# A fused attention and feed-forward kernel: the first sequence's attention written out in steps of two heads, with value copies behind exponentials and idle transposes between

## The chip, the cores and the metric

The kernel runs on one core of one Trainium2 chip. The metric is the device time of one execution in microseconds (us), lower is better. A core has five engines that concern us: TensorE (PE in the profile, with its weight loads as PEld), VectorE (DVE), ScalarE (ACT), GpSimd (POOL) and SyncE (SP). In the traces of the stage that is changed here, the instructions of each engine stand in the order in which the kernel writes them (TensorE's, from 39.51 us on, are shown below), and they wait for other engines by semaphores. "Granted clock" is the share of full speed that the throttle grants TensorE.

## The reference

Eight sequences, eight heads, 576 tokens, head size 64, all in fp32. Scores below the row's maximum minus tau are dropped before the softmax. The result goes through a feed-forward block of 512 to 2048 to 512 with an ELU between.

```python
scores = scale * np.matmul(q, k.transpose(0, 1, 3, 2))
thresh = np.max(scores, axis=-1, keepdims=True) - tau
scores = np.where(scores >= thresh, scores, -1000000000.0)
attn = np.exp(scores - np.max(scores, axis=-1, keepdims=True))
attn = attn / (np.sum(attn, axis=-1, keepdims=True) + 1e-09)
x = (attn @ v)            # then (B,H,S,D) -> (B*S, H*D)
h = x @ w_in
y = np.where(h > 0, h, np.exp(np.minimum(h, 0)) - 1) @ w_out
```

The weights arrive as float64 and are converted on the chip, piece by piece, with integer operations on VectorE, ScalarE and GpSimd.

## The kernel before

The change touches only the first sequence, which is computed before any feed-forward matmul can start. Its eight heads are four pairs of two, and a pair has five steps: four with 128 query rows of each of two heads, and a fifth with the 64 remaining rows of both heads in one tile. For every step there are scores on TensorE, a maximum on VectorE, a bias, an exponential on ScalarE, a mask on VectorE that also sums the row, and a normalising on GpSimd. Then TensorE transposes the weights (in parts, each copied out of PSUM by ScalarE), and multiplies them with the values, twice a pair. Before the change, this ran one head after another:

```python
def exponentials(pr, i, hs):
    ...
    nc.vector.tensor_reduce(st["mx"][:, cs], src[:, :, :, :HALF], axis=AX.XY, op=ALU.max)
    nc.gpsimd.tensor_scalar(st["nb"][:, cs], st["mx"][:, cs], nkeep, 1.0, ALU.mult, ALU.mult)
    ...
        nc.scalar.activation(e, st[h][:, :, :HALF], AF.Exp, bias=st["nb"][:, h : h + 1], scale=keep)

heads = [(pr, i, [h]) for pr, i in steps[:per_seq] for h in heads_of(i)]
begin(*heads[0])                              # scores and exponential
for n, (pr, i, hs) in enumerate(heads):
    if n + 1 < len(heads):
        begin(*heads[n + 1])                  # of the next head
    ...                                       # conversions of weights
    finish(pr, i, hs)                         # mask and normalise
    if len(turned) > 1:
        behind(*turned.popleft())             # values, when complete
    if n and hs == [0]:
        turn(*heads[n - 1][:2])               # transposes and their copies
        ...
```

Two pools in PSUM matter. Three buffers hold scores. Two banks, called rt, are shared by the transposed parts, by the products with the values (pv), and, in the changed kernel, by the idle transposes:

```python
def room():
    return psum["t"].tile([P, NC, P], FP32, name="rt", tag="rt")
# turn_parts of a two-head step: part 0 (4 chunks of one head), part 1 (4 chunks of the other), part 2 (the common chunk)
return [lambda: chunks(0, NC), lambda: chunks(NC + 1, NCH), lambda: chunks(NC, NC + 1)]
...
pv = psum["t"].tile([P, 512], FP32, name="pv", tag="rt")       # values: 2 passes with vd, then 16 with vm
```

## Time and profile before

| | |
|---|---|
| time, median of 3 (range) | 1388.53 us (1387.4 to 1390.45) |
| span in the profile, granted clock | 1384.1 us, 0.994 |
| first scores, first mask | 8.21 us, 13.13 us |
| scores of step 21, and their maximum | 105.55 us, 106.82 us |
| from that maximum to the end of the span | 1277.3 us |

The 21st step is the first one that both kernels write alike, so the start of its maximum is a marker: what stands before it belongs to the change, and what stands after should move as one block. I use this marker in every profile below. A timeline line gives start, duration, engine, source line, operation, output and inputs, shapes and count; in square brackets is how long the engine was idle before and what ended that.

### The profile page before, as it was taken

To read this page: it belongs to the slowest core of one execution; us is meant where nothing else is said; L and a number is where in the kernel's file an instruction comes from. 1 tells how busy PE (TensorE), PEld (TensorE's weight loads), DVE (VectorE), ACT (ScalarE), POOL (GpSimd) and SP (SyncE) were. 2 spreads that over 40 slices of the span, in tenths; PEclk is the share of its full clock that TensorE was granted. 3 is DMA by queue.
4 is the path that set the end of the run, shared out by engine and by line. 5 is a ranking of instruction groups with operands and counts; after the bars stand their busy time and mean duration, and the time that the engine had idled before them with its cause. 6 is when DMAs were issued, how large, how long until landed. Compare 5 with 4: busy or idle time off the path is not lost.

```text
span 1384.1 us, 21954 instructions
## 1 busy us (share of the span) xinstructions
PE 1334.5 (96%) x6566; PEld 988.6 (71%) x6566; DVE 1066.5 (77%) x2362; ACT 632.4 (46%) x1387; POOL 827.5 (60%) x1331
## 2 busy tenths in 40 slices
PE   6897989999999999999999999999999999999998
PEld 4554745747777777777777777777777777888886
DVE  6877885988888887888788978888888874545533
ACT  4666654325454445445453636263635452422421
POOL 5667773878657564756475747675666656414422
PEclk9999999999999999999999999999999999999999
DMA  5245451688897979898888988897889785411211
GB/s 114 58 91 148 132 148 44 187 244 254 226 261 221 280 214 255 209 266 240 230 231 256 251 222 236 236 258 212 239 230 275 217 241 146 133 58 64 92 57 31
DMA packets 316342, 259.82 MB, mean 188 GB/s; under 512 B 208320, under 2 KB 272320, under 8 KB 316224
## 3 DMA queue, kind: packets, MB, share of 16 engines
q1 hardware_dynamic: 316224, 258.42, 67.4%
q8 instruction: 53, 0.87, 0.3%
q14 instruction: 65, 0.53, 0.1%
HBM read 167.84 MB, written 90.51 MB: 187 GB/s over the span
## 4 chain that ended last, share of the span: by engine, by line
PE 76%; DVE 9%; ACT 5%; POOL 4%; issue 3%; DMA 1%; SPq 1%; DVEq 0%; POOLq 0%; ACTq 0%
PE f L999 28%; PE f L846 21%; PE sc L238 11%; PE pv L388 9%; PE pv L384 2%; PE f L435 2%; PE f L475 2%; ACT e L1088 2%; DVE w L265 2%; ACT e L253 1%; DVE mx L1078 1%; PE rt L277 1%; POOL wtop L143 1%; DVE mx L248 1%; DVE wtop L137 1%
## 5 line engine op out<-in xcount | busy, mean ns | idle before, releaser
L274 POOL TENSOR_SCALAR w<-w,rs 128x576 f32<-128x576 f32 x288 | 246.2, 860 | 108.4 <-DVE rs L1104 75.1
L1078 DVE TENSOR_REDUCE mx<-sc 128x1 f32<-128x576 f32 x207 | 148.0, 751 | 82.6 <-PE sc L238 82.6
L238 PE MATMUL sc<-kT,qT 64*128 64x288 f32 x1024 | 182.6, 440 | 22.1 <-DVE w L265 11.9
L348 DVE STREAM_TRANSPOSE x<-w 128x512 f32<-128x512 f32 (+1 forms) x350 | 182.5, 567 | 8.2 <-POOL w L274 8.2
L1086 ACT ACTIVATE nb<-mx,nkeep 128x1 f32<-128x1 f32 x207 | 61.4, 297 | 253.4 <-DVE mx L1078 253.4
L1088 ACT ACTIVATE e<-sc,nb,keep 128x576 f32<-128x576 f32 x207 | 172.1, 831 | 6.9
L1097 DVE SCALAR_TENSOR_TENSOR w<-sc,th,e 128x576 f32<-128x576 f32 x207 | 163.0, 810 | 8.6 <-ACT e L1088 0.4
L238 PEld LDWEIGHTS sc<-kT,qT 64*128 64x128 f32 x1024 | 100.7, 191 | 87.2 <-issue 51.8
L846 PE MATMUL f<-xt,sw 128*128 128x256 f32 x512 | 129.0, 389 | 1.0 <-DVE ot L1017 0.5
L846 PE MATMUL f<-xt,w_in_sb 128*128 128x256 f32 x512 | 125.1, 383 | 1.7 <-ACT w L860 1.5
L1082 POOL TENSOR_SCALAR th<-mx,ntau 128x1 f32<-128x1 f32 x207 | 54.3, 263 | 111.6 <-DVE mx L1078 111.4
L846 PEld LDWEIGHTS f<-xt,sw 128*128 128x128 f32 x512 | 93.2, 190 | 29.8 <-issue 13.5
L846 PE MATMUL f<-x,w_in_sb 128*128 128x256 f32 x448 | 109.0, 382 | 5.5 <-ACT g L913 5.5
L253 ACT ACTIVATE e<-sc,nb,keep 128x576 f32<-128x576 f32 x81 | 65.1, 830 | 104.2 <-POOL nb L249 103.2
L846 PEld LDWEIGHTS f<-xt,w_in_sb 128*128 128x128 f32 x512 | 95.7, 190 | 22.1 <-ACT xs L400 4.6
L999 PE MATMUL f<-w_out_sb,s 128*128 128x256 f32 x448 | 109.4, 387 | 0.0
L999 PE MATMUL f<-t,s 128*128 128x256 f32 x448 | 106.7, 381 | 0.6 <-POOL s L939 0.6
L999 PE MATMUL f<-w_out_sb,g 128*128 128x256 f32 x448 | 107.2, 382 | 0.0
L846 PEld LDWEIGHTS f<-x,w_in_sb 128*128 128x128 f32 x448 | 84.1, 190 | 21.2 <-ACT g L913 10.2
L999 PEld LDWEIGHTS f<-w_out_sb,s 128*128 128x128 f32 x448 | 82.3, 190 | 23.0 <-issue 13.2
L999 PEld LDWEIGHTS f<-w_out_sb,g 128*128 128x128 f32 x448 | 84.0, 190 | 15.8 <-ACT ge L879 3.5
L999 PEld LDWEIGHTS f<-t,s 128*128 128x128 f32 x448 | 84.0, 190 | 14.3 <-POOL s L939 3.4
(162 smaller groups left out, 2543.6 us busy)
## 6 DMA issues: line engine op xcount, KB each, us to landing
there<-x SPq DMA_DIRECT2D x500, 144.0 KB, 4.2
wTb<-there SPq DMA_DIRECT2D x75, 576.0 KB, 4.6
wTa<-there SPq DMA_DIRECT2D x50, 576.0 KB, 4.3
sw<-win_sums SPq DMA_DIRECT2D x62, 384.0 KB, 4.7
t<-wout_sums SPq DMA_DIRECT2D x45, 512.0 KB, 5.4
qm<-in_q_dram SPq DMA_DIRECT2D x128, 72.0 KB, 4.2
vm<-in_v_dram SPq DMA_DIRECT2D x64, 128.0 KB, 4.2
wst<-in_moe_w_in_dram SPq DMA_DIRECT2D x16, 512.0 KB, 4.5
```

The source lines that it names most:

```text
L238: nc.tensor.matmul(scs[h][:, a, :HALF], qs[r], kT[r, k0 : k0 + HALF], start=True, stop=True)
L253: nc.scalar.activation(e, st[h][:, :, :HALF], AF.Exp, bias=st["nb"][:, h : h + 1], scale=keep)
L274: nc.gpsimd.tensor_scalar(wv, wv, st["rs"][:, h : h + 1], 1.0, ALU.mult, ALU.mult)
L348: nc.vector.transpose(x[:, :, c0 : c0 + nc_], src.rearrange("p (c g n) -> p g c n", c=nc_, n=T))
L388: nc.tensor.matmul(pv[h * D : (h + 1) * D, g0 * T : g1 * T], vm[:, h, c], wT[:, g0:g1, h * (NC + 1) + c], start=False, stop=(c == NC - 1), ...
L846: nc.tensor.matmul(loc["banks"][place], left[:, j], right[:, j], start=(begins and j == 0), stop=(j == 1), skip_group_check=True)
L999: nc.tensor.matmul(place(m), lhs, rhs, start=(begins and v == 0), stop=(v == RU - 1), skip_group_check=True)
L1078: nc.vector.tensor_reduce(st["mx"][:, h : h + 1], st[h][:, :, :HALF], axis=AX.XY, op=ALU.max)
L1082: nc.gpsimd.tensor_scalar(st["th"][:, h : h + 1], st["mx"][:, h : h + 1], 1.0, ntau, ALU.mult, ALU.add)
L1086: nc.scalar.mul(st["nb"][:, h : h + 1], st["mx"][:, h : h + 1], nkeep)
L1088: nc.scalar.activation(e, st[h][:, :, :HALF], AF.Exp, bias=st["nb"][:, h : h + 1], scale=keep)
L1097: nc.vector.scalar_tensor_tensor(wv, sc[:, :, :HALF], st["th"][:, h : h + 1], e, ALU.is_ge, ALU.mult, accum_out=st["sm"][:, h : h + 1])
```

## The change

The intent is to take the waits between engines out of the first stage. The stage is now written in a fixed order by steps of two heads. The biases of the first heads go to ScalarE. The copies of the values' products and of the transposed parts stand behind the exponentials, so that ScalarE starts these first. TensorE gets idle transposes, which transpose the identity into a buffer nobody reads, to keep its clock up: 28 at the start, then 6 and 9 in three of the five steps. The first loads of k are issued by ScalarE beside those of q by SyncE. The core of it (`...` marks what is left out):

```diff
-    for n, (pr, i, hs) in enumerate(heads):
-        if n + 1 < len(heads):
-            begin(*heads[n + 1])
...
+        load(0, ("km",), queue=nc.scalar)
...
+        def idle(n):
+            rt = psum["t"].tile([P, NC, P], FP32, name="rt", tag="rt")
+            for _ in range(n):
+                transpose(rt[:, 0], ident)
+
+        idle(28)
...
+            if n:
+                normalize(*steps[n - 1], [0])
+                turned = turn_parts(*steps[n - 1])
+                if i in (0, 1, 3):
+                    idle(6)
+            max_of(pr, i, 0)
+            exp_of(pr, i, 0)
+            bound_of(pr, i, 0)
+            if n:
+                copies = turned[0]()
...
+                exp_of(pr, i, 1, True)
+                bound_of(pr, i, 1)
+            if out_values:
+                out_values()
+            if n and i < NB - 1:
+                copies()
...                                   (conversions, q and k of the next pair)
+            mask_of(pr, i, 0)
+            if i in (0, 1, 3):
+                idle(9)
+            if n + 1 < per_seq:
+                scores(*steps[n + 1], heads_of(steps[n + 1][1]))
+            if n:
+                for part in turned[1:]:
+                    part()()
+            if len(hs) == 2:
+                mask_of(pr, i, 1)
+            reciprocal_of(pr, i, hs)
+            out_values = None
+            if n > 1 and steps[n - 2][1] in (1, NB - 1):
+                out_values = values(steps[n - 2][0], 0 if steps[n - 2][1] == 1 else 1)
```

So TensorE's line in a step n is: 6 idle, part 0 of step n-1, 9 idle, scores of step n+1, parts 1 and 2 of step n-1, and in the second and fourth step of a pair, last, the values of the step before that. The idle ones are there in a pair's first, second and fourth steps.

More of the change, by code (lines that the diff above doesn't have):

```diff
@@ L78, with read_tau @@
     tau_sb = const.tile([P, 1], FP32, name="tau_sb")
-    nc.sync.dma_start(tau_sb, tau.to_broadcast([P, 1]))
-    pos = const.tile([P, 1], FP32, name="pos")
-    nc.vector.tensor_scalar(pos, tau_sb, 0.0, None, ALU.is_ge)
-    keep = const.tile([P, 1], FP32, name="keep")
-    nc.vector.tensor_scalar(keep, pos, SCALE, None, ALU.mult)
-    nkeep = const.tile([P, 1], FP32, name="nkeep")
-    nc.vector.tensor_scalar(nkeep, pos, -SCALE, None, ALU.mult)
-    far = const.tile([P, 1], FP32, name="far")
-    nc.vector.tensor_scalar(far, pos, -FAR, FAR, ALU.mult, ALU.add)
-    ntau = const.tile([P, 1], FP32, name="ntau")
-    nc.vector.tensor_tensor(ntau, tau_sb, far, ALU.max)
-    nc.vector.tensor_scalar(ntau, ntau, -1.0 / SCALE, None, ALU.mult)
+    pos, keep, nkeep, far, ntau = (const.tile([P, 1], FP32, name=x) for x in ("pos", "keep", "nkeep", "far", "ntau"))
+    def read_tau():
+        nc.vector.tensor_scalar(pos, tau_sb, 0.0, None, ALU.is_ge)
+        nc.vector.tensor_scalar(keep, pos, SCALE, None, ALU.mult)
+        nc.vector.tensor_scalar(nkeep, pos, -SCALE, None, ALU.mult)
+        nc.vector.tensor_scalar(far, pos, -FAR, FAR, ALU.mult, ALU.add)
+        nc.vector.tensor_tensor(ntau, tau_sb, far, ALU.max)
+        nc.vector.tensor_scalar(ntau, ntau, -1.0 / SCALE, None, ALU.mult)
     w_in_sb = const.tile([P, KJ, DF], FP32, name="w_in_sb")
@@ L131, in convert_top, with convert_shift @@
     def convert_top(i):
+        convert_shift(i)
+        convert_sign(i)
+    def convert_shift(i):
         if i in staged:
@@ L136, in convert_top, with convert_sign @@
             nc.vector.tensor_scalar(top, hi, 3, 0x3FFFFFFF, ALU.logical_shift_left, ALU.bitwise_and)
+    def convert_sign(i):
+        if i in staged:
+            hi, top = staged[i][:, :, 1], tops[i]
             nc.vector.scalar_tensor_tensor(top, hi, 0xC0000000, top, ALU.bitwise_and, ALU.bitwise_or)
@@ L155, in convert_end, with load @@
             nc.vector.scalar_tensor_tensor(pieces[i][1], mag, 1.125 * 2.0**-15, top, ALU.is_ge, ALU.mult)
-    def convert_w():
-        i = progress[1]
-        if i >= progress[0]:
-            return
-        for f in (convert_top, convert_rest, convert_add, convert_abs, convert_end):
-            f(i)
-        load_w()
     raws, pairs = {}, {}
-    def load(pr, parts=("qm", "km", "v"), shared=False):
+    def load(pr, parts=("qm", "km", "v"), shared=False, queue=nc.sync):
         b, j = divmod(pr, NPAIR)
@@ L178, in load @@
                     r = (2 * i + d) * T
-                    nc.sync.dma_start(
+                    queue.dma_start(
                         m[r : r + T],
@@ L238, in scores @@
                 nc.tensor.matmul(scs[h][:, a, :HALF], qs[r], kT[r, k0 : k0 + HALF], start=True, stop=True)
-        if len(hs) == 2 and not apart:
+        if len(hs) == 2 and "f" in psum and not apart:
             st["both"] = both
@@ L274, in normalize, with max_of, bound_of, exp_of @@
             nc.gpsimd.tensor_scalar(wv, wv, st["rs"][:, h : h + 1], 1.0, ALU.mult, ALU.mult)
+    def max_of(pr, i, h):
+        st = open_steps[pr, i]
+        nc.vector.tensor_reduce(st["mx"][:, h : h + 1], st[h][:, :, :HALF], axis=AX.XY, op=ALU.max)
+    def bound_of(pr, i, h):
+        st = open_steps[pr, i]
+        nc.gpsimd.tensor_scalar(st["th"][:, h : h + 1], st["mx"][:, h : h + 1], 1.0, ntau, ALU.mult, ALU.add)
+    def exp_of(pr, i, h, on_pool=False):
+        st = open_steps[pr, i]
+        if not on_pool:
+            nc.scalar.mul(st["nb"][:, h : h + 1], st["mx"][:, h : h + 1], nkeep)
+        e = att.tile([P, 2, HALF], FP32, name="e")
+        nc.scalar.activation(e, st[h][:, :, :HALF], AF.Exp, bias=st["nb"][:, h : h + 1], scale=keep)
+        st[h] = st[h], e
+    def mask_of(pr, i, h):
+        st = open_steps[pr, i]
+        if h == 0:
+            st["w"] = wpool[0].tile([P, 2 * S], FP32, name="w")
+        sc, e = st.pop(h)
+        wv = st["w"][:, h * S : (h + 1) * S].rearrange("p (a n) -> p a n", a=2)
+        nc.vector.scalar_tensor_tensor(wv, sc[:, :, :HALF], st["th"][:, h : h + 1], e, ALU.is_ge, ALU.mult,
+                                       accum_out=st["sm"][:, h : h + 1])
+    def reciprocal_of(pr, i, hs):
+        st = open_steps[pr, i]
+        cs = slice(hs[0], hs[-1] + 1)
+        nc.vector.tensor_scalar(st["sm"][:, cs], st["sm"][:, cs], 1e-9, None, ALU.add)
+        nc.vector.reciprocal(st["rs"][:, cs], st["sm"][:, cs])
     def transpose(dst, src):
@@ L288, in turn_parts @@
     def turn_parts(pr, i):
-        w = open_steps.pop((pr, i))["w"]
+        w = open_steps[pr, i]["w"]
         wT, g0 = turned_tile(pr, i)
@@ L537, in finish_units @@
                 post()
-    def begin(*step):
-        scores(*step)
-        exponentials(*step)
-    def finish(*step):
-        masks(*step)
-        normalize(*step)
-    def ahead(pr, i):
-        if i == 2 and pr + 1 < NP:
-            prep(pr + 1)
-        if i == 3 and pr + 2 < NP:
-            load(pr + 2, ("qm", "km"))
-        if i == 3 and pr + 1 < NP and pr:
-            load(pr + 1, ("v",))
-    load(0)
-    prep(0)
-    load(1)
-    heads = [(pr, i, [h]) for pr, i in steps[:per_seq] for h in heads_of(i)]
@@ L560 @@
-    turned = deque()
-    begin(*heads[0])
-    for n, (pr, i, hs) in enumerate(heads):
-        if n + 1 < len(heads):
-            begin(*heads[n + 1])
-        if n == 2:
-            load_w()
-            load_w()
-        if n >= 12 and n % 4 == 0:
-            convert_w()
-        finish(pr, i, hs)
-        if len(turned) > 1:
-            behind(*turned.popleft())
-        if n and hs == [0]:
-            turn(*heads[n - 1][:2])
-            turned.append(heads[n - 1][:2])
-        if hs == [1]:
-            ahead(pr, i + 1)
+    with tc.manual_schedule():
+        load(0, ("qm",))
+        nc.sync.dma_start(tau_sb, tau.to_broadcast([P, 1]))
+        load(0, ("km",), queue=nc.scalar)
+        load(0, ("v",))
+        load(1)
+        def idle(n):
[3 more added lines that the diff above has]
+        idle(28)
+        prep_q(0)
+        prep_k(0)
+        read_tau()
+        copy_k(0)
+        copy_q(0)
+        scores(0, 0, [0, 1])
+        out_values = None
+        for n in range(per_seq):
+            pr, i = steps[n]
+            hs = heads_of(i)
+            x = progress[1]
+            if n:
[9 more added lines that the diff above has]
+            if len(hs) == 2:
+                max_of(pr, i, 1)
+                st = open_steps[pr, i]
+                nc.gpsimd.tensor_scalar(st["nb"][:, 1:], st["mx"][:, 1:], nkeep, 1.0, ALU.mult, ALU.mult)
+            if n and len(heads_of(steps[n - 1][1])) == 2:
+                normalize(*steps[n - 1], [1])
+            if len(hs) == 2:
+                exp_of(pr, i, 1, True)
[4 more added lines that the diff above has]
+                copies()
+            if i == NB - 1 and n + 1 < per_seq:
+                convert_top(x)
+                convert_add(x)
+                convert_abs(x)
+                convert_rest(x + 1)
+            elif i == 0 and n:
+                convert_end(x)
+                load_w()
+            elif i == 1 and pr:
+                convert_sign(x)
+                convert_add(x)
+            elif i in (2, 3):
+                (prep_q if i == 2 else prep_k)(pr + 1)
+                (copy_q if i == 2 else copy_k)(pr + 1)
+            if i == NB - 1:
+                copies()
+            mask_of(pr, i, 0)
[6 more added lines that the diff above has]
+                    part()()
+            if len(hs) == 2:
+                mask_of(pr, i, 1)
+            reciprocal_of(pr, i, hs)
+            out_values = None
+            if n > 1 and steps[n - 2][1] in (1, NB - 1):
+                out_values = values(steps[n - 2][0], 0 if steps[n - 2][1] == 1 else 1)
+            if i == 0 and n:
+                convert_shift(x + 1)
+            elif i == 2 and pr:
+                convert_end(x)
+                load_w()
+            if i == 1 and pr:
+                convert_abs(x)
+            if i == 2 and n + 3 < per_seq:
+                convert_rest(progress[1])
+            if i in (3, 4):
+                load(pr + 2, ("qm",) if i == 3 else ("km",))
+            if i == 3 and pr:
+                load(pr + 1, ("v",))
+            if n == 0:
+                load_w()
+                load_w()
+        for h in heads_of(steps[per_seq - 1][1]):
+            normalize(*steps[per_seq - 1], [h])
@@ L580 @@
         psum[name] = banks.enter_context(tc.tile_pool(name=f"ps_{name}", bufs=bufs, space=PSUM))
-    while len(turned) > 1:
-        behind(*turned.popleft())
     SWITCH = (NPAIR + 3) * NB
@@ L1074, in ffn_quarters @@
                 n -= 1
-        def max_of(pr, i, h):
-            st = open_steps[pr, i]
-            nc.vector.tensor_reduce(st["mx"][:, h : h + 1], st[h][:, :, :HALF], axis=AX.XY, op=ALU.max)
-        def bound_of(pr, i, h):
-            st = open_steps[pr, i]
-            nc.gpsimd.tensor_scalar(st["th"][:, h : h + 1], st["mx"][:, h : h + 1], 1.0, ntau, ALU.mult, ALU.add)
-        def exp_of(pr, i, h):
-            st = open_steps[pr, i]
-            nc.scalar.mul(st["nb"][:, h : h + 1], st["mx"][:, h : h + 1], nkeep)
-            e = att.tile([P, 2, HALF], FP32, name="e")
-            nc.scalar.activation(e, st[h][:, :, :HALF], AF.Exp, bias=st["nb"][:, h : h + 1], scale=keep)
-            st[h] = st[h], e
-        def mask_of(pr, i, h):
-            st = open_steps[pr, i]
-            if h == 0:
-                st["w"] = wpool[0].tile([P, 2 * S], FP32, name="w")
-            sc, e = st.pop(h)
-            wv = st["w"][:, h * S : (h + 1) * S].rearrange("p (a n) -> p a n", a=2)
-            nc.vector.scalar_tensor_tensor(wv, sc[:, :, :HALF], st["th"][:, h : h + 1], e, ALU.is_ge, ALU.mult,
-                                           accum_out=st["sm"][:, h : h + 1])
-        def reciprocal_of(pr, i, hs):
-            st = open_steps[pr, i]
-            cs = slice(hs[0], hs[-1] + 1)
-            nc.vector.tensor_scalar(st["sm"][:, cs], st["sm"][:, cs], 1e-9, None, ALU.add)
-            nc.vector.reciprocal(st["rs"][:, cs], st["sm"][:, cs])
         begun = [0.0]
```

## The prediction

> **What bounds the kernel now.** I read the page's slices first. TensorE is busy in nine tenths or more of nearly every slice from the seventh on, and only the first three slices (some 105 us) show it at 6, 8 and 9 tenths with VectorE at 6, 8 and 7. The change touches only the attention of the first sequence: four head pairs of five steps each (four steps of two heads, a fifth of one head), before any feed-forward matmul. Next I placed that stage in the timeline: first scores at 8.21 us, the scores of step 21, which the change leaves alone, at 105.55 us. From there on both kernels have the same written order. The busy time by stretches (stretch, length, then busy and count of TensorE, its weight loads, VectorE, ScalarE, GpSimd; granted clock, DMA share, GB/s) says:
>
> ```profile
> 8.20:105.60 97.40, 89.30 (x436) 53.32 (x436) 74.96 (x208) 63.03 (x125) 60.76 (x128) 0.96 0.40 88
> ...
> 60.00:64.00 4.00, 2.81 (x12) 1.57 (x11) 3.67 (x11) 2.40 (x5) 2.33 (x8) 1.00 0.00 0
> 64.00:68.00 4.00, 4.00 (x11) 2.58 (x11) 2.35 (x9) 2.27 (x4) 2.13 (x5) 0.51 0.00 0
> 68.00:72.00 4.00, 4.00 (x18) 1.43 (x17) 2.19 (x8) 0.83 (x1) 2.21 (x5) 0.64 0.00 0
> ```
>
> No engine is full: VectorE has 75 of 97 us, ScalarE 63, and TensorE's 89 includes matmuls drawn out by pipelining and a slow clock. So the stage is bound by waits between engines. The waits of this stretch (waiter, releaser, us in total, times, longest):
>
> ```profile
> ACT e L253 <- POOL nb L249: 28.6, 19, 9.8
> POOL nb L249 <- DVE mx L248: 12.6, 7, 4.4
> DVE mx L248 <- PE sc L238: 10.8, 12, 2.4
> ```
>
> This is the loop scores, maximum, bias, exponential, run head by head, with GpSimd's small bias and normalising in between. The timeline gives its terms, and the clock's effect on TensorE (start, duration, instruction, idle before):
>
> ```profile
> 8.21 4.20 PE L238 MATMUL sc<-kT,qT 64*128 64x288 f32 x12 [8.21 <-DVE kT L200]
> ...
> 17.23 1.97 PE L277 MATMUL rt<-ident,w 128*128 128x128 f32 x8
> ...
> 47.27 1.09 PE L277 MATMUL rt<-ident,w 128*128 128x128 f32 x8
> ...
> 60.06 0.80 DVE L265 SCALAR_TENSOR_TENSOR w<-sc,th,e 128x576 f32<-128x576 f32 x1
> ...
> 60.93 1.23 PE L238 MATMUL sc<-kT,qT 64*128 64x288 f32 x4 [0.45 <-DVE w L265]
> ...
> 700.76 1.24 PE L238 MATMUL sc<-kT,qT 64*128 64x288 f32 x8
> ...
> 702.03 1.42 DVE L1078 TENSOR_REDUCE mx<-sc 128x1 f32<-128x576 f32 x2 [0.97 <-PE sc L238]
> ...
> 702.82 0.29 ACT L1086 ACTIVATE nb<-mx,nkeep 128x1 f32<-128x1 f32 x1 [1.26 <-DVE mx L1078]
> ...
> 703.15 0.83 ACT L1088 ACTIVATE e<-sc,nb,keep 128x576 f32<-128x576 f32 x1
> ```
>
> The reader should see: mask to next scores 0.87 us (60.06 to 60.93); scores to maximum 1.27; maximum to bias 0.79; bias to exponential 0.33; the exponential 0.83. Exponential to mask adds 0.11 (another place: exponential at 61.00, mask at 61.94). Eight transposes took 1.97 us early and 1.09 later, and the clock fell once, at 64 us.
>
> **The Trainium skill.** "TensorE: Matmul & The Clock Gate", Part 1 (the HAM clock gate): half clock until a window of some 3.4 us has been busy, half again after an idle one. The trace agrees in the halving (1.97 against 1.09 us, and 0.51 granted at 64 us), though it lists 1.00 for the early stretch whose durations are doubled. Part 4 of that page (PE-mode transpose) says transposes do not count as busy in the same way; if so, idle transposes alone warm nothing. No run shows it yet. "DMA: Bandwidth & Descriptors", Specifications: full rate needs transfers of 512 B or more; in the first 20 us 12430 of 12686 packets are smaller, at 143 GB/s. The same page, Issuing engines are not separate DMA queues: issuing from a second engine saves only issue time. The trace agrees as far as it goes: DMA share is 0.7 to 0.8 from 8 to 20 us.
>
> **The start.** k's four loads move to ScalarE's queue, beside q's. Before, SyncE issued them one after another, half a microsecond each, from 1.18 to 5.39 us, and k was transposed at 7.38. Now all are issued by about 2.8 us. But q and k are 590 KB in 128-byte pieces, data flow from about 2.1 us, and at 140 GB/s that takes until 6.3 us. Two transposes (0.7 and 0.8 us) then give scores at 7.5 instead of 8.21. The 28 idle transposes, at 0.2 us cold, end by 7.0 and delay nothing; if they warm the clock, the maximum follows 1.27 us after the scores where it took 2.32 (8.21 to 10.53). First mask: 7.5 + 1.27 + 0.79 + 0.33 + 0.83 + 0.11 = 10.8 us, against 13.13 before. About 2.3 us won, 1.05 of it from warmth.
>
> **The loop by steps of two heads.** No work is removed: 36 exponentials, 36 masks, 36 maxima, 36 normalisings, six weight pieces converted, as before. Twenty of the 36 biases go from GpSimd to ScalarE. Added are 28 idle transposes at first and 6 + 9 in three of five steps. With three score buffers, the first head's first matmul of the next step need not wait for this step's first mask, so the maximum comes about 0.24 us earlier than the chain above: 0.87 + 1.03 + 0.79 + 0.33 + 0.83 + 0.11 = 3.96 us from first mask to first mask. VectorE alone, by distances between starts: two masks 1.48, accumulator, sum and reciprocal 0.40, two maxima 1.42, together 3.3; a q or k transpose adds 0.69, and a conversion 0.42, 0.69 and 0.68. ScalarE alone: bias 0.33, exponentials 1.5, copies 0.5, 0.5, 0.27, together 3.1; values' copies 0.37 or 0.79, a converted piece 0.56 twice.
>
> I walked one later pair by hand, each engine in its written order, from first mask to first mask. First to second step: VectorE, 1.88 + 0.42 + 1.42 + 0.69 = 4.41. Second to third: ScalarE does two copies and a conversion's absolute value after the scores, so the bias waits until 3.6 after the mask instead of 2.69; with 0.33 + 0.83 + 0.11 this is 4.88. Third to fourth: part two of the values (2.9 us of TensorE) began late, because its buffer waits for a copy, so the scores start 1.5 us after the mask; then ScalarE has three value copies, three score copies and a conversion before the bias, which comes at 4.45: 5.7. Fourth to fifth: the one-head scores stand ready, 1.88 + 0.79 + 0.33 + 0.83 + 0.11 = 3.94. Fifth to the next first: ScalarE again (values' copy, two conversion passes, three copies), 4.27. A pair takes 23.2 us. The first pair has no values before its fourth step and almost no conversions, 21.4; the last has four intervals and one conversion pass less, 18.4. Sum 21.4 + 2 x 23.2 + 18.4 = 86.2 us from first to last mask. The idle transposes (0.11 us each when warm, at most 1.8 us a step) fit in TensorE's waits: by my walk they end 0.4 us before the mask lets the scores go in the second step, and just as it does in the first.
>
> End of the stage: 10.8 + 86.2 + 0.9 (mask to the scores of step 21) = 97.9; I add 1.0 for the second mask, whose bound stands behind a normalising on GpSimd and comes up to 0.15 us late per two-head step. That is 98.9 against 105.55: 6.6 us less. Everything after moves rigidly. 1388.5 - 6.6 = 1382.
>
> **Rivals.** First, the stage reaches VectorE's bound: 75 us of work after 8.6 us, ending near 92 with small gaps, a gain of 12 us or 1376. For it: VectorE's own sum is under each step. Against it: ScalarE's one queue holds the next bias behind copies in three of five steps. Second, idle transposes stand in TensorE's way or warm nothing: at a cold 0.22 us, fifteen take 3.3 us in a step of 4 to 5 that also has up to 5 us of real work; TensorE becomes the bound, the gain vanishes, 1388 or even 1392. Against it: real matmuls then fill the window and warm the clock, as at 19 and 72 us. Third, the saving is absorbed later by a wait for weights: the next stage needs pieces 7 and 8, and loads of 512 KB land in about 4.6 us but are issued three steps, some 14 us, ahead. I think this weak, worth 1 us.
>
> **Range and chances.** The whole stage is 97 of 1388 us; even at VectorE's bound the gain is under 1%. So within 2% is nearly certain. Prediction 1382 us, range 1376.5 to 1387.5, which runs from the first rival to nearly none of the gain.
>
> **What would show it.** First scores near 7.5 us with eight matmul passes in about 1.2 us (warm) or 2.3 (cold); no granted clock near 0.5 before 100 us; the scores of step 21 near 99 us; the waits of the bias, now on ScalarE, shortened, with the third step of later pairs the longest, at 5.7 us. The prediction is wrong if the stage ends before 94 or after 104 us, or if the time between step 21 and the end, now 1278.5 us, changes by over 2 us.

## The result, and the profile after

| | before | after |
|---|---|---|
| time, median (range), 4 runs each on one chip | 1389.49 (1387.4 to 1391.05) | 1391.18 (1388.93 to 1392.89) |
| span of the profiled execution | 1384.1 | 1387.1 |
| first scores, first mask | 8.21, 13.13 | 8.13, 11.47 |
| maximum of step 21 | 106.82 | 109.60 |
| from there to the end | 1277.3 | 1277.5 |

The ratio of times is 1.0012, with a 95% interval of 0.9989 to 1.0035. Ratios here are the mean time of one kernel's fast runs over the mean of the other's in the same rounds, so not quite the ratio of the medians. A later round of 22 runs gave 1.0016 (1.0008 to 1.0024). The kernel is some 1.5 to 2.2 us slower, where 6.5 us less was predicted: the same within 2%, and outside the predicted range. All runs of this study are in the fast state. (The profiled execution of before, 1385.93 us, was quicker than its timed ones, that of after the quickest of its four, so the spans differ by a little more than the medians.)

The marker in the two timelines, before and then after:

```profile
106.82 1.36 DVE L248 TENSOR_REDUCE mx<-sc 128x2 f32<-128x1152 f32 x1 [2.48 <-PE sc L238]
```

```profile
109.60 1.36 DVE L245 TENSOR_REDUCE mx<-sc 128x2 f32<-128x1152 f32 x1 [3.40 <-PE sc L235]
```

The stage ends 2.8 us later, and the rest takes 1277.5 us against 1277.3. So 2.8 of the 3.0 us between the two profiled spans lie in the stage that was changed. (The rest is not so rigid in every execution: over all thirteen profiles of this study it took 1277.3 to 1281.7 us, and 1279.6 in a second profile of this same kernel. So I compare stages by the marker.) Busy time by stretches after (stretch, length, busy and count of TensorE, weight loads, VectorE, ScalarE, GpSimd; granted clock, DMA share, GB/s):

```profile
8.10:108.30 100.20, 89.57 (x608) 62.26 (x608) 77.91 (x182) 67.89 (x145) 57.42 (x110) 1.00 0.42 86
...
64.00:68.00 4.00, 3.43 (x22) 2.41 (x21) 3.62 (x10) 2.48 (x6) 3.47 (x6) 1.00 0.00 0
68.00:72.00 4.00, 4.00 (x28) 2.03 (x28) 3.18 (x9) 3.12 (x8) 2.03 (x6) 1.00 0.00 0
```

The recorded clock is 1.00 all through, where the kernel before fell to 0.51 and 0.64 between 64 and 72 us. The durations agree: nine idle transposes take 1.20 us at 9.68 us and 1.15 at 49.78 and at 100.50. TensorE has 608 matmul records in the stage, 436 before, and is busy as long as before although nothing is slowed any more. The start of the timeline after:

```profile
1.46 5.24 PE L305 MATMUL rt<-ident 128*128 128x128 f32 x28 [1.46 <-POOL ident masks.py:199]
...
8.13 1.62 PE L235 MATMUL sc<-kT,qT 64*128 64x288 f32 x8 [1.44 <-DVE pos L82]
...
9.40 1.42 DVE L275 TENSOR_REDUCE mx<-sc 128x1 f32<-128x576 f32 x2 [0.60 <-PE sc L235]
```

The first maximum follows the scores by 1.27 us, as predicted for a warm clock, and the first mask comes 1.66 us earlier than before. Yet from this mask to the marker the changed kernel takes 98.1 us (11.47 to 109.60), and the kernel before 93.7 (13.13 to 106.82). The gain of the start is given back in the loop, and 2.8 us more. What do the engines wait for there? The longest waits of the stage after:

```profile
POOL w L271 <- PE rt L305: 10.8, 6, 2.5
ACT wTa L321 <- PE rt L305: 9.9, 8, 1.6
...
ACT nb L284 <- DVE mx L275: 8.1, 2, 6.0
ACT xt L423 <- PE pv L416: 8.0, 7, 1.5
...
DVE mx L275 <- PE sc L235: 7.3, 6, 1.8
```

The 28.6 us in which ScalarE's exponential waited for GpSimd's bias are gone. Of the bias's 8.1 us, now on ScalarE, 6.0 are the wait for the very first maximum. Most of the long waits now name TensorE as the one that is late (of the two left out above 8.0 us, one is GpSimd's wait for VectorE's reciprocal, 9.2). The chain of work that ended last, cut to 30 to 60 us (second pair and a little on each side), says it in one line; before, and then after:

```profile
by line: PE sc L238 14.7%; PE pv L388 13.9%; PE rt L277 12.4%; issue 9.8%; DVE w L265 7.9%; DVE mx L248 7.9%; POOL nb L249 4.9%; POOL w L274 4.4%; ACT e L253 4.3%; POOL wtop L143 4.2%; PE pv L384 3.0%; DVE qT L195 2.6%; POOL th L250 2.3%; D
```

```profile
by line: PE rt L305 44.1%; PE sc L235 24.0%; PE pv L416 15.4%; ACT wTb L321 5.9%; PE pv L412 5.4%; ACT wTa L321 4.0%; issue 1.5%
```

Before, TensorE holds 44% of the chain and the rest is spread over all engines. After, it holds 89%, VectorE and GpSimd are off the chain, and the only other engine on it is ScalarE with the copy that gives an rt buffer back. The timeline shows how this looks from the second pair's second step (its first mask is at 39.02 us) to its fourth (50.46):

```profile
39.51 1.62 PE L235 MATMUL sc<-kT,qT 64*128 64x288 f32 x8
41.06 0.77 PE L305 MATMUL rt<-ident,w 128*128 128x128 f32 x5
41.76 0.75 ACT L321 COPY wTa<-rt 128x512 f32<-128x512 f32 x2 [1.39 <-PE rt L305]
42.40 0.91 PE L412 MATMUL pv<-wTb,vd 128*128 128x384 f32 x2 [0.57 <-ACT wTa L321]
43.24 2.37 PE L416 MATMUL pv<-wTb,vm 128*64 128x320 f32 x16
44.20 0.82 DVE L295 SCALAR_TENSOR_TENSOR w<-sc,th,e 128x576 f32<-128x576 f32 x1 [0.74 <-POOL th L279]
45.54 0.66 PE L305 MATMUL rt<-ident,w 128*128 128x128 f32 x4
46.13 1.24 PE L235 MATMUL sc<-kT,qT 64*128 64x288 f32 x8
...
48.63 0.87 PE L305 MATMUL rt<-ident 128*128 128x128 f32 x6 [0.57 <-ACT wTa L321]
49.34 0.60 PE L305 MATMUL rt<-ident,w 128*128 128x128 f32 x4
49.78 1.15 PE L305 MATMUL rt<-ident 128*128 128x128 f32 x9
50.76 1.14 PE L235 MATMUL sc<-kT,qd 128*128 128x288 f32 x4
...
53.01 0.70 PE L412 MATMUL pv<-wTa,vd 128*128 128x256 f32 x2 [0.57 <-ACT wTb L321]
```

The mask that "lets the scores go" came at 44.20 us; the scores stood in line behind the values and part 0 and came at 46.13. Values stand between two scores twice a pair, and each time they wait first for a ScalarE copy to free their buffer. Between 48.63 and 50.76 lie fifteen idle transposes, ahead of the one-head scores, the parts behind them and the values. All idle transposes of the stage's steps together (the group of this line and tile: count, then busy us and mean ns):

```profile
L305 PE MATMUL rt<-ident 128*128 128x128 f32 x174 | 23.2, 275 | 4.0 <-ACT wTa L321 2.3 <-ACT wTb L321 1.7
```

By their starts they come 0.11 us apart (nine in the 0.98 us from 49.78 to 50.76), so by my estimate 174 of them fill some 19 us of a line that is the bound.

The intervals between first masks of steps in the second pair, from their starts 34.65, 39.02, 44.20, 50.46, 54.36 and 59.87:

| interval | predicted | after |
|---|---|---|
| first to second step | 4.41 | 4.37 |
| second to third | 4.88 | 5.18 |
| third to fourth | 5.7 | 6.26 |
| fourth to fifth | 3.94 | 3.90 |
| fifth to next first | 4.27 | 5.51 |
| sum | 23.2 | 25.2 |

### The profile page after: what moved, and what is told of

Same layout as the page of the kernel before. It is cut to its first block, busy times and chain, and to the rows that moved or that the text cites. A ratio compares the mean times of both kernels' runs of the same rounds, so it can differ in the third digit from the quotient of the medians.

```text
span 1387.1 us, 22282 instructions
## 1 busy us (share of the span) xinstructions
PE 1340.4 (97%) x6768; PEld 1002.2 (72%) x6768; DVE 1068.6 (77%) x2330; ACT 637.1 (46%) x1407; POOL 822.9 (59%) x1311
## 4 chain that ended last, share of the span: by engine, by line
PE 76%; DVE 9%; ACT 5%; POOL 3%; DMA 3%; issue 3%; SPq 1%; ACTq 0%; DVEq 0%; POOLq 0%
PE f L1085 28%; PE f L932 20%; PE sc L235 11%; PE pv L416 8%; PE rt L305 3%; PE pv L412 2%; PE f L463 2%; PE f L503 2%; ACT e L286 2%; DVE mx L275 2%; DMA there<-x 1%; DVE w L262 1%; DVE w L295 1%; ACT e L250 1%; POOL wtop L148 1%
## 5 line engine op out<-in xcount | busy, mean ns | idle before, releaser
L275 DVE TENSOR_REDUCE mx<-sc 128x1 f32<-128x576 f32 x243 | 173.5, 751 | 89.4 <-PE sc L235 89.3
L295 DVE SCALAR_TENSOR_TENSOR w<-sc,th,e 128x576 f32<-128x576 f32 x243 | 191.5, 811 | 19.9 <-POOL th L279 5.2
L286 ACT ACTIVATE e<-sc,nb,keep 128x576 f32<-128x576 f32 x243 | 200.6, 831 | 8.0 <-POOL nb L607 0.2
L284 ACT ACTIVATE nb<-mx,nkeep 128x1 f32<-128x1 f32 x227 | 67.4, 297 | 261.8 <-DVE mx L275 261.8
L235 PE MATMUL sc<-kT,qT 64*128 64x288 f32 x1024 | 165.5, 432 | 13.0 <-DVE w L262 9.1
L235 PEld LDWEIGHTS sc<-kT,qT 64*128 64x128 f32 x1024 | 92.2, 187 | 73.0 <-issue 50.1
L279 POOL TENSOR_SCALAR th<-mx,ntau 128x1 f32<-128x1 f32 x243 | 64.5, 266 | 119.6 <-DVE mx L275 119.1
L932 PEld LDWEIGHTS f<-xt,sw 128*128 128x128 f32 x512 | 93.2, 190 | 29.8 <-issue 13.5
L951 POOL TENSOR_TENSOR u<-u,w 128x256 f32<-128x256 f32 x64 | 49.1, 768 | 69.2 <-ACT u L946 65.7
```

The source lines that it names most:

```text
L235: nc.tensor.matmul(scs[h][:, a, :HALF], qs[r], kT[r, k0 : k0 + HALF], start=True, stop=True)
L275: nc.vector.tensor_reduce(st["mx"][:, h : h + 1], st[h][:, :, :HALF], axis=AX.XY, op=ALU.max)
L279: nc.gpsimd.tensor_scalar(st["th"][:, h : h + 1], st["mx"][:, h : h + 1], 1.0, ntau, ALU.mult, ALU.add)
L284: nc.scalar.mul(st["nb"][:, h : h + 1], st["mx"][:, h : h + 1], nkeep)
L295: nc.vector.scalar_tensor_tensor(wv, sc[:, :, :HALF], st["th"][:, h : h + 1], e, ALU.is_ge, ALU.mult, accum_out=st["sm"][:, h : h + 1])
L932: nc.tensor.matmul(loc["banks"][place], left[:, j], right[:, j], start=(begins and j == 0), stop=(j == 1), skip_group_check=True)
```

## The experiments

My theory after reading the two traces was that TensorE's written line is the bound (idle transposes, part 0, scores, parts, copy, values), so that whatever is added to it or taken from it shows in full. Its rivals: that ScalarE's order is the bound, as my walk had it in three of five steps (S); and, on the idle transposes, that they are what holds the clock (W), or that they only stand in the line and cost time (A). All kernels are edits of the changed one, gave a correct result, and are timed against the kernel before. Medians of the kernel before on the chips concerned were 1389.4 (27 runs), 1389.9 (55) and 1389.6 (44).

### No idle transposes in the steps

```diff
                 turned = turn_parts(*steps[n - 1])
-                if i in (0, 1, 3):
-                    idle(6)
...
             mask_of(pr, i, 0)
-            if i in (0, 1, 3):
-                idle(9)
```

> The changed kernel without the 6 and 9 idle transposes in the steps; the 28 at first stay. Marker: the start of the maximum of step 21 (109.60 us in the changed kernel, 106.82 before). Theory A (idle transposes stand in front of the fourth step's one-head scores, and so delay the values and the next first step): fifth-to-first interval falls from 5.5 to about 4.6 us, marker about 3.5 us earlier, near 106; no cold stretch. Rival W (they hold the clock): the granted clock falls to about 0.5 somewhere before 105 us and the marker is not earlier than 109, perhaps 112.

Measured: 1398.56 us median (5 runs), ratio 1.0069 (1.0056 to 1.0082); marker at 120.45 us. Three stretches of its profile:

```profile
36.00:40.00 4.00, 2.59 (x14) 1.39 (x12) 3.45 (x10) 3.03 (x7) 1.15 (x3) 1.00 0.00 0
40.00:44.00 4.00, 2.62 (x15) 1.56 (x14) 3.69 (x7) 2.96 (x7) 3.31 (x6) 0.99 0.01 2
44.00:48.00 4.00, 3.54 (x11) 1.46 (x9) 2.70 (x7) 2.21 (x5) 3.17 (x8) 0.50 0.01 2
```

The clock is at 0.50 from 44 to 48 us, and there are cold stretches (0.50 in the middle) within 12 to 32, 68 to 80 and 92 to 112 us too. The step transposes hold the clock, as W says, and the stage without them is 10.9 us longer. It was not one long gap that lost it: in the 8 us before 44 TensorE never stood still for more than 0.87 us, but it was busy for only 5.2 of them. Where the clock was full, the interval from the fifth to the next first step was 4.60 us (60.48 to 65.08) instead of 5.51: this much of A is right.

### No idle transposes at all

```diff
-        idle(28)
```

(and the two removals above)

> As the run without step idles, and without the 28 idle transposes at first too. If transposes warm the clock: first maximum comes 2.3 us after the first scores instead of 1.27, TensorE runs at half rate to about 19 us, marker 2 to 4 us later than in the run that keeps the 28. If transposes do not count as work for the clock: no difference over 0.3 us.

Measured: 1400.41 us (6 runs), ratio 1.0082 (1.0066 to 1.0098); marker at 117.89. Its start, first without any idle transposes, then the one with the 28 alone (the run above):

```profile
8.40 3.24 PE L235 MATMUL sc<-kT,qT 64*128 64x288 f32 x10 [8.40 <-DVE pos L82]
...
10.72 1.42 DVE L275 TENSOR_REDUCE mx<-sc 128x1 f32<-128x576 f32 x2 [1.65 <-PE sc L235]
```

```profile
8.14 1.72 PE L235 MATMUL sc<-kT,qT 64*128 64x288 f32 x10 [1.02 <-DVE pos L82]
```

The same ten passes take 3.24 us and 1.72, and the maximum comes 2.32 us after the scores where the changed kernel has 1.27. So transposes of the identity alone do warm the clock (they are fp32 here), and the start's 1.05 us from warmth is as predicted. The record gives 1.00 as granted clock from the start of this run up to 64 us, although these first passes ran at half speed: before its first change, the recorded clock alone is no evidence. One expectation was missed: the marker came 2.6 us earlier than in the run with the 28 (117.89 against 120.45), and not 2 to 4 later. The cold spells of the two profiled executions differ (the second pair took 24.2 us in this one and 27.1 in the other), and this one was the quickest of its six runs, the other the slowest of its five, so the two markers do not measure the start; the intervals of the two ratios overlap.

### ScalarE's conversions and copies moved

The conversion passes of ScalarE are put ahead of the copies or into other steps, so that no bias stands behind a conversion and three copies (the core of the edit).

```diff
-            if out_values:
-                out_values()
-            if n and i < NB - 1:
-                copies()
             if i == NB - 1 and n + 1 < per_seq:
                 ...
                 convert_abs(x)
-                convert_rest(x + 1)
             elif i == 0 and n:
+                convert_rest(x + 1)
+            elif i == 2 and pr:
+                convert_abs(x)
+            elif i == 3 and n + 2 < per_seq:
+                convert_rest(x)
+            if out_values:
+                out_values()
+            if n and i < NB - 1:
+                copies()
```

> The changed kernel with all its idle transposes, but ScalarE's conversion passes written behind the exponentials of the next step (or, in the fifth step, before the values' copy, where ScalarE idles) so that none stands before a bias. Theory S (ScalarE's order holds the next bias): in later pairs second-to-third interval falls from 5.2 to 4.6, third-to-fourth from 6.26 to 5.7, fifth-to-first from 5.5 to 5.1; marker 4 to 5 us earlier, near 105. Rival (TensorE's order alone sets these intervals): under 1 us.

Measured: 1392.36 us (22 runs), ratio 1.0016 (1.0008 to 1.0023); marker at 109.57, 0.03 us from the changed kernel. A later pair takes 4.37, 4.63, 6.24, 4.38 and 5.60, again 25.2 in sum. ScalarE did hold the second interval (5.18 before, 4.63 now), but what it gains the fourth and fifth lose. So S falls for this kernel: ScalarE's order moves time between its steps and does not set the pair's length.

### Both edits

> No step idles and ScalarE's passes moved. If A and S are both right and independent: marker near 101 to 102, 5 us before that of the kernel before, time ratio about 0.9965. If they are the same wait seen twice: near 105. If W holds: a cold stretch and no gain.

Measured: 1398.19 us (5 runs), ratio 1.0063 (1.0051 to 1.0075); marker at 117.11, with cold stretches at 12 to 32, 40 to 56 and 92 to 104 us. It tells nothing of S beyond the run before, since the clock rules it.

### No idle transposes in the fourth step alone

```diff
-                if i in (0, 1, 3):
+                if i in (0, 1):
                     idle(6)
...
-            if i in (0, 1, 3):
+            if i in (0, 1):
                 idle(9)
```

> The changed kernel without the 6 + 9 idle transposes of the fourth step only; those of the first and second steps stay. Theory A2 (TensorE's written order sets the pair: idle transposes, scores, a score copy and the values stand in one line before the next first scores, and those of the fourth step are the only ones that do not end before a mask): fifth-to-first interval of later pairs 5.5 to 4.6 us, marker (maximum of step 21) 3 to 4 us earlier than 109.60, if the clock stays. Rival W2 (any hole of that size drops the clock): granted clock 0.5 in a stretch of each pair, marker later than 109.60, as in the run without step idles (120.45).

Measured: 1388.14 us (20 runs), ratio 0.9988 (0.9979 to 0.9996); marker at 107.79, so 1.8 us earlier than the changed kernel. In the second pair, from its timeline:

```profile
51.89 0.82 DVE L295 SCALAR_TENSOR_TENSOR w<-sc,th,e 128x576 f32<-128x576 f32 x1 [0.96 <-POOL kT L209]
...
53.54 0.70 PE L412 MATMUL pv<-wTa,vd 128*128 128x256 f32 x2 [0.15 <-ACT wTb L321]
```

The values start 1.65 us after the fourth step's mask (51.89 to 53.54), where the changed kernel has 2.55 (50.46 to 53.01), and the interval from the fifth step to the next first is 4.61 and, a pair later, 4.97, instead of 5.51. These fifteen transposes were in the way. (They also take two turns in the ring of rt buffers, but part 0 now waits 0.66 us for a copy where the idle ones waited 0.57, so it is their time that was saved.) In the first pair, where no values fill TensorE yet, the clock fell to 0.72 and 0.50 between 20 and 28 us, and the interval there stayed at 5.60; so the gain is below the 0.9 us a pair that the warm pairs show. That their absence made it fall is not shown: it fell at about 21.7 us, before the first of them would have been issued (23.41 in the changed kernel), and it fell at the same place in two runs below that keep them (the short part first, and k on SyncE).

### The values made longer

```diff
-        nc.tensor.matmul(pv[:, :n], vd, wT[:, :, NC], start=True, stop=False, skip_group_check=True)
+        for _ in range(times):
+            nc.tensor.matmul(pv[:, :n], vd, wT[:, :, NC], start=True, stop=False, skip_group_check=True)
...
-                out_values = values(steps[n - 2][0], 0 if steps[n - 2][1] == 1 else 1)
+                out_values = values(steps[n - 2][0], 0 if steps[n - 2][1] == 1 else 1, 3)
```

Each product with the values begins with a matmul that overwrites; issuing it three times leaves the result right and lengthens TensorE's line by a known piece.

> The changed kernel with the first matmul of each values' group issued three times in the first sequence (each overwrites the last, the result is right): 0.7 us more of TensorE in each of four first parts and 0.9 us in each of three second parts, 5.5 us in all. If the values stand on the path between two scores, as theory A2 has it, all of it passes through: marker near 115. If the stage is set by VectorE or ScalarE and the values have slack, under 1.5 us.

Measured: 1398.38 us (4 runs), ratio 1.0061 (1.0042 to 1.008); marker at 116.97, which is 7.37 us later. The two lengthened pieces in the second pair, in the timeline:

```profile
43.29 2.20 PE L413 MATMUL pv<-wTb,vd 128*128 128x384 f32 x6 [0.56 <-ACT wTa L321]
...
55.20 1.56 PE L413 MATMUL pv<-wTa,vd 128*128 128x256 f32 x6 [0.57 <-ACT wTb L321]
```

In the changed kernel these two pieces took 0.91 and 0.70 us, so 1.29 and 0.86 were added; with three of the first kind and four of the second in the stage that is 3 x 1.29 + 4 x 0.86 = 7.3 us. (My expectation had put the addition at 5.5 us.) All of it comes out at the end, and it comes out where it was put in: the third-to-fourth interval grew from 6.26 to 7.55 us, the fifth-to-first from 5.51 to 6.37. If VectorE or ScalarE had been the bound with TensorE waiting, part of it would have been swallowed. The theory of TensorE's line stands.

### The short part first

```diff
-                for part in turned[1:]:
+                for part in turned[:0:-1]:
                     part()()
```

> The changed kernel with the one common transpose written before the four of the second half, so that the buffer that the values take is freed by the short copy (0.27 us) and not by the long one (0.58 us). By theory A2 values start 0.6 to 0.7 us earlier in seven places: marker 4 us earlier, near 105.5. If the values' start is not on the path: no change over 0.5 us.

Measured: 1385.61 us (18 runs), ratio 0.9968 (0.9959 to 0.9977); marker at 105.23, 4.4 us earlier than the changed kernel and 1.6 earlier than before. No work is removed. The values' product takes the rt buffer that the last part but one leaves. In the written order that is part 1, four chunks, whose copy (0.59 us) can't begin until four transposes are done; now it is the single common chunk:

```profile
41.83 0.27 ACT L321 COPY wTa<-rt 128x128 f32<-128x128 f32 x1 [1.01 <-PE rt L305]
42.15 0.91 PE L412 MATMUL pv<-wTb,vd 128*128 128x384 f32 x2
```

The values start 2.24 us after the scores of this step (39.91 to 42.15) where the changed kernel has 2.89 (39.51 to 42.40). Seven times 0.65 is 4.6 us, close to the 4.4 measured, but in part by luck: the second and third pairs are 1.6 us shorter each, and the first lost about 1 us to a cold spell (0.69 of the clock at 20 to 24 us; its third-to-fourth interval 6.26 for 5.22), without which the gain would be some 5.4 by this estimate. The pair's intervals, by first masks at 35.14, 39.42, 44.56, 50.15, 54.06 and 58.79, are 4.28, 5.14, 5.59, 3.91 and 4.73.

### Short part first, and no idle transposes in the fourth step

> Both: no idle transposes in the fourth step and the common transpose first. By A2 the two add: marker near 102, 4 to 5 us before that of the kernel before (106.82), ratio near 0.9965. With a cold stretch (W2): later than 106.

Measured: 1386.25 us (21 runs), ratio 0.9978 (0.997 to 0.9986); marker at 104.25, intervals of a later pair 4.28, 5.14, 5.59, 3.91 and 4.74. The two do not add up. The last interval is the same with the fourth step's idle transposes (4.73) and without (4.74), so once the values start early, taking these transposes out no longer brings the next pair's scores forward. With them, TensorE's own line holds the chain in the fourth step (47.13 to 50.20 us in the run before). Without them, another engine holds it about as long:

```profile
50.61 0.66 PE L305 MATMUL rt<-ident,w 128*128 128x128 f32 x4 [1.28 <-ACT wTb L321]
```

TensorE waits 1.28 us there for a ScalarE copy, and the chain that ended last is ScalarE's from 47.16 to 50.57 us (a copy, a conversion pass, the bias, two exponentials, a copy). So ScalarE's order, which set nothing in the changed kernel, is the next limit by this chain. The marker is 1.0 us earlier and the median 0.6 us later than with the short part alone; this profile too has a cold stretch, at 21.5 to 25 us, and the intervals of the two ratios overlap.

### The three together, with the idle transposes kept in the first pair

```diff
-                if i in (0, 1, 3):
+                if i < 2 or pr == 0 and i < 4:
                     idle(6)
...
-            if i in (0, 1, 3):
+            if i < 2 or pr == 0 and i < 4:
                 idle(9)
...
-                for part in turned[1:]:
+                for part in turned[:0:-1]:
```

(and ScalarE's passes moved as above)

> Common transpose first; idle transposes in the first and second steps, and in the third and fourth of the first pair alone, where no values fill TensorE; ScalarE's passes moved behind the exponentials. With TensorE's line shortened, ScalarE's order should now count where it counted nothing alone (theory A2 with S as the next limit): later pairs 23.7 us (no idles in the fourth step, common first) to about 22; no cold stretch before 100 us; marker near 100 to 101; ratio near 0.995. Rival: ScalarE's order has slack in this kernel too, or the clock drops: marker 103 or later.

Measured: 1383.38 us (7 runs, 1382.72 to 1388.44), ratio 0.9961 (0.9947 to 0.9975); intervals of a later pair 4.30, 4.58, 5.58, 4.14 and 4.76.

```profile
8.10:101.70 93.60, 87.44 (x580) 59.19 (x580) 77.58 (x181) 68.77 (x145) 57.14 (x110) 1.00 0.43 91
```

```profile
102.95 1.36 DVE L245 TENSOR_REDUCE mx<-sc 128x2 f32<-128x1152 f32 x1 [2.27 <-PE sc L235]
```

The marker is 6.7 us earlier than in the changed kernel and 3.9 earlier than before, and no stretch before it is cold. I had hoped for 100 to 101 and a pair of about 22 us; the pair took 23.4, and the marker is next to the rival's 103. The first pair, now without a cold spell, took 22.0 us for 23.1 in the run before; the second and third only 0.3 less each, and the last 0.3 more. In the fourth step ScalarE still holds the chain, from 46.15 to 49.55 us. Nor did the whole gain reach the end of this profile: its span is 1384.6 us, in part because TensorE waited 3.1 us later on for transfers (wTa<-there, there<-x), which it did not do in the profiles of the two kernels. (The profiled run, 1386.52 us, is one of the three slower of the seven.) In the times this version is faster than both kernels, by 0.4% of the kernel before, which is still within 2%; that it is faster than the short part first alone (0.9968) is not shown.

### k's first loads on SyncE again

```diff
-        load(0, ("km",), queue=nc.scalar)
+        load(0, ("km",))
```

> The changed kernel with k's first four loads on SyncE's queue behind q's and tau's, as before the change. If the transfers and not their issue set the start (the trace shows q landing at 6.64 us where it landed at 5.41 alone): first scores within 0.4 us of 8.13, marker within 0.4 us of 109.60. If the second queue was worth what I predicted: first scores 0.7 us later or more.

Measured: 1393.16 us (20 runs), ratio 1.0024 (1.0016 to 1.0032). First scores at 8.78 us instead of 8.13, so the second issuing engine is worth 0.65 us there, more than the 0.4 I had allowed for transfers alone and just under the 0.7 for the full effect. In this run q, alone at first, landed earlier (4.62 us against 6.64), and k was transposed later (7.95 against 7.34). The profiled execution lost its clock at 20 to 29 us (0.68 and 0.50), so its marker at 113.06 is not the queue's doing alone; in the times the difference is within the intervals (1.0024 against 1.0016 for the changed kernel in the same rounds).

### The changed kernel again

> The changed kernel unchanged, beside the others on the same chip: times in two bands near 1389.3 and 1392.7 us, ratio to before near 1.0015; marker 109.6.

Measured: 1391.07 us (22 runs, 1389.16 to 1394.35), ratio 1.0016 (1.0008 to 1.0024); marker at 109.74. The runs fall into two bands, 1389.2 to 1391.4 us at a mean clock of 0.996 to 0.998 and 1392.4 to 1394.4 at 0.994 to 0.996. That the upper one has one more cold spell fits the two clocks, and the first pair with the cold spell in the run before took 2.8 us longer (25.98 for 23.17); but no profile of an upper run of this kernel was set beside a lower one, so this is not shown.

## Why the prediction was right or wrong

**The start.** Half right. Warmth was worth what I said: maximum 1.27 us after the scores. The scores came at 8.13 and not 7.5. q's data landed at 6.64 us, not by 6.3, and from there to the first scores it took 1.49 us, two transposes in a row. (My own terms, 6.3 + 0.7 + 0.8, give 7.8 and not 7.5.) The first mask at 11.47 was 0.67 late.

**The loop, where VectorE or the ready scores set the step.** Right: first to second 4.37 for 4.41, fourth to fifth 3.90 for 3.94.

**The loop, second to fourth step.** The step of the prediction that says "ScalarE does two copies and a conversion's absolute value after the scores, so the bias waits" was right for that one interval, which fell by 0.55 us when those passes were moved, and wrong as what sets the pair, which stayed at 25.2 us. "Part two of the values ... began late, because its buffer waits for a copy" was the right mechanism, with a size too small: the scores came 1.93 us after the mask (44.20 to 46.13) instead of 1.5. That this wait sets the pair is shown by the short part put first, which takes 4.4 us off the stage.

**The fifth step.** This is the term with the largest error per pair: 5.51 for 4.27. The failed step is "the idle transposes ... fit in TensorE's waits". I checked it for the first and second steps and not for the fourth, where they delay the one-head scores, which delays the parts, the copy, the values and the next scores. Without them the interval was 4.61. In more general terms, the walk gave TensorE waits to fill in every step, where its own written line had become the bound: 89% of the chain from 30 to 60 us, and all 7.3 us that were added to it came out at the end.

**The end.** I put 0.9 us from the last mask to the scores of step 21. The changed kernel needed 3.34 (104.99 to 108.33), with values, eight transposes and a copy in the line first. The kernel before needs 2.97 (102.58 to 105.55), so its own trace would have said so.

**The sum.** Measured against the bare walk of 97.9 (the extra 1.0 for bounds is not needed), the scores of step 21 are 10.4 us late: 0.7 from the start, 1.8 from the first pair (23.2 for 21.4), 4.4 from two middle pairs (25.2 and 25.6, for 23.2 each), 1.1 from the last (19.5 for 18.4), 2.4 from the end. (One reading was loose: the page's fourth and sixth slices, with TensorE at 7 and 8 tenths, are not full either, and they lie outside the stage.)

**Rivals.** The first (VectorE's bound) did not come: VectorE is off the chain. (Its sum was loose, too: 8.6 + 75 is 84 us, so that the 92 allowed 8 us of gaps, and from 105.55 to 92 is 13.5 us and not 12.) The second came in part: its figure of 1388 to 1392 is what was measured, but its reason was a cold clock, and the idle transposes keep the clock warm and stand in the way nevertheless, so the figure came right for another reason. The third (a later wait for weights) did not come in the changed kernel: the rest took 1277.5 us against 1277.3. (A wait of this kind, for other transfers, took 3.1 us of the gain in the profile of the three edits together.)

**What stays open.** The idle transposes still fill a part of a line that is the bound, and without them the clock falls. How few would do was tried in a few settings only. Why the version with everything together missed its expectation by about 2 us is only narrowed down: its chain names ScalarE in the fourth step, and no further edit tested that. Why the clock fell at 21 to 22 us in some profiles, and not in others with the same instructions up to there, is open too.

## What to carry to other kernels

When one engine's queue is written by hand, walk that queue alone first, instruction after instruction, and only then the loop between engines: an instruction that "fits in a wait" costs its full length wherever the queue has no wait left. Where several kinds of tile share a small ring of buffers, put the short-lived one where the next user inherits it; here that reordering alone was worth 4.4 us. Filler that warms a clock was worth having here (without it in the steps the stage ended 10.9 us later), but it cost time in a step whose queue had no wait left.

## What the Trainium skill lacked or had wrong

- "TensorE: Matmul & The Clock Gate", Part 4 (PE-mode transpose), says that full clock doesn't engage for transposes. Here 28 fp32 transposes of the identity alone warmed it (ten passes in 1.72 us instead of 3.24), and the step transposes held 1.00 where without them 0.50 was granted.
- The same page, Part 1 (The HAM clock gate), ties the fall to an idle window, and its later section on a second failure mode to frequent short idling, without a share. Here it fell after 8 us with no gap above 0.87 us and TensorE busy for 5.2 us.
- The same page's caveat calls the clock's trace events unreliable. The runs show one way: 1.00 is listed from the start to the first change, in one run up to 64 us, although its first passes, at 8.40 us, ran at half speed.
- "DMA: Bandwidth & Descriptors", Issuing engines are not separate DMA queues, calls the saved issue time usually small beside the transfer. That is not contradicted, but at a kernel's start it can be worth having: here the second queue brought the first scores from 8.78 to 8.13 us.
- No page says what filler in an in-order queue costs when needed work stands behind it: here 0.9 us a pair, of fifteen transposes at 0.11 us (and nothing, 4.73 us against 4.74, once the values started earlier, where ScalarE held the step as long).
